# The last two units of an attention-and-FFN kernel: which thirds of x are turned by DMA, where one eviction stands, and when row sums are made

## The chip, the cores and the metric

The kernel runs on one core of one Trainium2 chip. A core has five engines that run side by side and meet through semaphores: TensorE (PE in the profile; its weight loads are shown apart as PEld), VectorE (DVE), ScalarE (ACT), GpSimd (POOL) and SyncE (SP, which here only issues DMAs). The metric is the device time of one execution in microseconds; less is better. A run is told by the median of its executions, and one execution is profiled. The profile's span is the time from the first to the last instruction of the program.

## The reference

Two blocks, one behind the other. First an attention with a hash mask: a query may see a key only if the signs of six projections agree. Then a gated FFN with RMS norm on the result, 3072 rows of 512.

```python
# B, H, S, D = 4, 8, 768, 64
mask = q_bucket[:, :, :, None] == k_bucket[:, :, None, :]      # sign bits of q @ proj, k @ proj
scores = np.where(mask, scale * np.matmul(q, k.transpose(0, 1, 3, 2)), -1000000000.0)
attn = softmax(scores)                                          # + 1e-09 in the denominator
x = np.matmul(attn, v).transpose(0, 2, 1, 3).reshape(B * S, H * D)

rms = np.sqrt(np.mean(x * x, axis=-1, keepdims=True) + 1e-06)
xn = x / rms * rms_g
g = xn @ w_gate
silu = g * (1.0 / (1.0 + np.exp(-g)))
out = (silu * (xn @ w_val)) @ w_out
```

## The kernel before

**Units and slots.** The work is cut into 8 units of 384 rows: unit `u` is half of batch element `u // 2`, and its 384 rows are three thirds `c` of 128. A unit's attention is 8 heads of 3 chunks, so 24 slots (`NS`). In a slot PE makes the scores of the next chunk (`scores`, L345, tile `s_ps`, two buffers) and ACT the exponentials of this one (`probs`, L357, tile `psb`). Everything else is filled into the slots by a plan: `plan[t]` is a list of steps, run in its order behind the scores and exponentials of slot `t`. All engines take their instructions in the order in which the plan emits them.

**What a unit goes through.** `av` (L370) multiplies the exponentials with v into `o_ps`, two heads (a pair) in one tile, of which there is one buffer. `attn_out` (called by `o_step`) empties it: DVE adds a constant and writes `otmp` (L384), takes reciprocals `rcp` (L389), and POOL multiplies into `x` (L391) and squares into `sq` (L397). `sumsq` (called by `s_step`, L413) sums the rows of `sq` on DVE. Behind the last pair, `norm` makes the row scale (`ss` on DVE, `rstd` on POOL) and scales x to `xn` in fp16.

Then `xn` must be turned, so that features lie on partitions (`xnT`), third by third, in one of two ways. `turn_dma` (L427) issues a DMA transpose on SP's queue; for such a third `norm` multiplies the RMS weights in along the row (`grow`, L448). `turn_x` makes four TensorE transposes into a PSUM bank (L463, tile `x_ps`), and the eviction multiplies the RMS weights in (`gcol`): one instruction on DVE (L469) or, with `act=True`, four on ACT (L467); for such a third `norm` multiplies by the row scale alone (`norm_third`, L456). The table `ONDMA` says how many thirds of a unit go by DMA.

The FFN has 12 tiles `ft` of 128 hidden features. `gate` (L480, `g_ps`) and `value` (L480, `v_ps`) are four matmuls each over `xnT`, in two parts; all four read all three thirds of `xnT`. ACT makes a tanh `t` of the gate (L488), DVE makes `a` from `t` and `g_ps` (L497) and `ht` from `a` and `v_ps` (L498). `project` (L509, `y_ps`) multiplies `ht` with the output weights, 12 matmuls for a third, and `store` copies on ACT (L521) and stores on SP (L522). `g_ps`, `v_ps`, `y_ps` and `x_ps` share three PSUM banks.

**Where a unit's steps run.** In unit `u + 1`'s 24 slots run, for units below 7, `norm(u)`, the turning of its x, `project` of unit `u - 1`, and the gates and values of unit `u`. `spread` places the projections, turns and gates over the slots by weights (`SCORES`, `AV`, `PROJ`, `FEED`, `TURN`): a slot takes pieces until its share of the total weight is used. `o_step` comes one slot behind the second `av` of a pair begins, `s_step` some slots later. Where such a step falls outside the first two units, and not into slot 2 or 4 of a unit, it goes to the list `late`, which is appended to the plan behind everything that `spread` placed: it then stands behind the gates of its slot.

**The tail.** After the last slot come the last rest of the plan (the last `av` steps and the `o_step` of unit 7's last pair, on DVE) and then, written out by hand: the projections of unit 6, in between them `norm(7)` and the turning of unit 7's x by `turn_x`, then unit 7's gates and values, its projections and stores.

In the run before, unit 6's attention lies from about 222 to 257 us of the span, unit 7's from about 257 to 292 us, and the tail behind it.

Of the kernel before, what the change touches and what calls it, by code (L numbers as in the profile page):

```python
# [21 lines left out]
NF = DFF // 128  # L22
# [11 lines left out]
def kernel(  # L34
# [12 lines left out]
    nc = tc.nc  # L47
# [36 lines left out]
    def bank(name, shape=None, dt=FP32):  # L84
        return gps.tile(shape or [128, 512], dt, name=name, tag="g")
# [326 lines left out]
    def sumsq(u, hp, sq):  # L412
        nc.vector.tensor_reduce(  # L413
            out=ssp[u % 2][:, hp, :], in_=sq, op=ALU.add, axis=AX.X
        )
# [3 lines left out]

    rstds = {}  # L420

    ONDMA = {2: 2, 3: 2, 4: 2, 5: 2, 6: 3}

    def turn_dma(u, c):
        if c == 0:
            xnT[u] = npool.tile([128, 4, HALF], FP16, name="xnT", bufs=2)
        nc.sync.dma_start_transpose(  # L427
            out=xnT[u][:, :, c * 128 : (c + 1) * 128], in_=xn[u][:, c, :]
        )


    def norm_scale(u):

        ss = spool.tile([128, 3], FP32, name="ss")
        nc.vector.tensor_reduce(
            out=ss, in_=ssp[u % 2].rearrange("p h c -> p c h"), op=ALU.add, axis=AX.X
        )
        rstd = spool.tile([128, 3], FP32, name="rstd")
        nc.gpsimd.tensor_tensor(out=rstd, in0=ss, in1=mhalf, op=ALU.pow)
        rstds[u] = rstd  # L440

    def norm(u):
        if u not in rstds:
            norm_scale(u)
        xn[u] = npool.tile([128, 3, DMODEL], FP16, name="xn")
        for c in range(3 if u else 2):
            if c < ONDMA.get(u, 0):
                nc.vector.scalar_tensor_tensor(  # L448
                    out=xn[u][:, c, :], in0=x[u][:, c, :], scalar=rstds[u][:, c : c + 1],
                    in1=grow, op0=ALU.mult, op1=ALU.mult,  # L450
                )
            else:
                norm_third(u, c, nc.vector.tensor_scalar_mul)

    def norm_third(u, c, mul):
        mul(xn[u][:, c, :], x[u][:, c, :], rstds[u][:, c : c + 1])  # L456

    def turn_x(u, c, act=False):
        if c == 0:
            xnT[u] = npool.tile([128, 4, HALF], FP16, name="xnT", bufs=2)  # L460
        ps = bank("x_ps", [128, 4, 128], FP16)
        for kt in range(4):
            nc.tensor.transpose(ps[:, kt, :], xn[u][:, c, kt * 128 : (kt + 1) * 128], ident16)  # L463
        dst = xnT[u][:, :, c * 128 : (c + 1) * 128]
        if act:
            for kt in range(4):
                nc.scalar.mul(dst[:, kt], ps[:, kt], gcol[:, kt : kt + 1])  # L467
        else:
            nc.vector.tensor_mul(dst, ps, gcol.unsqueeze(2).to_broadcast([128, 4, 128]))  # L469
# [34 lines left out]
    def project(u, c, f0, f1):  # L504
        if f0 == 0:
            obank[u, c] = bank("y_ps")
        y = obank[u, c]
        for ft in range(f0, f1):
            nc.tensor.matmul(  # L509
                y, ht[u][:, ft, c * 128 : (c + 1) * 128], wo[:, ft, :],  # L510
                start=(ft == 0), stop=(ft == NF - 1),
            )

    def rows_of(u, c):
        b, half = divmod(u, 2)
        rows = out[b * S : (b + 1) * S, :].rearrange("(p c) n -> p c n", c=6)
        return rows[:, 2 * c + half if b in PARITY else 3 * half + c, :]

    def store(u, c):
        ysb = spool.tile([128, DMODEL], FP32, name="ysb", bufs=3)  # L520
        nc.scalar.copy(ysb, obank.pop((u, c)))  # L521
        nc.sync.dma_start(out=rows_of(u, c), in_=ysb)  # L522
# [65 lines left out]
    NS = 24  # L588
# [5 lines left out]
    def at(w, s, f, *a):  # L594
        plan[NS * w + s].append(lambda: f(*a))
# [125 lines left out]
    def s_step(u, hp):  # L721
# [3 lines left out]
        else:  # L725
            sumsq(u, hp, sq)

    late = []
    for n, (u, h) in enumerate(order):
        t = 3 * n + 4 - ((u, h) == (0, H - 1))  # L730
        for part in range(2):
            at(0, t + part, av, u, h, part)
        if h % 2:
            if (u, h) == (0, H - 1):

                at(0, t + 1, o_step, u, h // 2, nc.vector)
                at(0, t + 1, norm_scale, u)
                at(0, t + 1, nc.vector.tensor_scalar_mul, gcol, gcol, float(DMODEL) ** 0.5)
                at(0, t + 2, hash_only, 1, 1)
                at(0, t + 2, hash_signs, 1, 1)  # L740
                at(0, t + 2, norm, u)
                at(0, TX-1, norm_third, u, 2, nc.scalar.mul)
                at(0, TX + 1, send_pair, 1, 1)
                for c in range(3):
                    at(0, TX, turn_x, u, c, c == 2)
                continue
            if (u, h) == order[-1]:
                at(0, t + 1, o_step, u, h // 2, nc.vector)
                continue

            steps = [(t + 1, o_step), (t + (6 if h < 7 else 3), s_step)]
            for s, step in steps:
                if s < 2 * NS or s % NS in (2, 4):
                    at(0, s, step, u, h // 2)
                else:
                    late.append((s, step, u, h // 2))
# [58 lines left out]
    for u in range(7):  # L815
        gates = [
            (FEED, f is gate and part == 0, [(0, f, u, ft, part)])
            for ft in range(NF) for f in (gate, value) for part in range(2)
        ]
        if u == 0:  # L820
            t0 = TX + 1
            spread(t0, 2 * NS - t0, gates)
            continue
        t0 = NS * (u + 1)
        at(0, t0 + 4, norm, u)
        for c in range(ONDMA.get(u, 0)):
            at(0, t0 + 5, turn_dma, u, c)
        pieces = []
        for i in range(9):
            c, n = divmod(i, 3)  # L830
            steps = [(0, project, u - 1, c, 4 * n, 4 * n + 4)]
            if n == 2:
                steps.append((1, store, u - 1, c))
            pieces.append((4 * PROJ, True, steps))
            if i in (6, 7):
                thirds = ((0,), (1, 2))[i - 6]
                for c in thirds:
                    if c >= ONDMA.get(u, 0):
                        pieces.append((TURN, False, [(0, turn_x, u, c)]))
                    elif u < 6:  # L840
                        pieces.append((TURN, False, []))
        lag, after = LAGS[u - 1 : u + 1]
        spread(t0 + lag, NS + after - lag, pieces + gates)
# [6 lines left out]
    def behind_norm(t):  # L850

        return t - t % NS + 9 if 1 <= t % NS < 9 else t

    for (b, hp), (load, kturns, qturns, _) in spots.items():
# [3 lines left out]
        for w, turns in (("k", kturns), ("q", qturns)):  # L858
            for i, t in enumerate(turns):
                at(0, t, turn_dve, b, hp, w, i, len(turns))  # L860
            t = turns[-1] + 1
            at(0, t if (b, hp) == (1, 2) else behind_norm(t), cast_pool, b, hp, w)
        t = 54 if (b, hp) == (1, 2) else behind_norm(qturns[-1] + 2)
# [16 lines left out]
    for t in range(LAST, LAST + 6):  # L880
        for f in plan[t]:
            f()
    for c in range(2):
        project(6, c, 0, NF)
        store(6, c)
    norm(7)
    project(6, 2, 0, 4)
    for c, f0, f1 in ((0, 4, 6), (1, 6, 8), (2, 8, NF)):
        turn_x(7, c, c == 1)
        project(6, 2, f0, f1)  # L890
    store(6, 2)
    for ft in range(NF):
# [37 lines left out]
```

## Time and profile before

| | us |
|---|---|
| median of 3 runs | 328.9 (328.4 to 329.17) |
| the profiled execution | 328.83 |
| its span | 326.7 |
| PE busy in the span | 321.3 (98%) |
| ACT, DVE, POOL busy | 228.3, 231.2, 157.6 |

PE's mean granted clock is 1.000. Rows of the timeline show start, length, engine, line, operation, what it writes and reads, and how many instructions were merged; in brackets stands the idle time of the engine before it and what ended it, if that was more than a little. A matmul's length covers its run through the array, so that one can start while the one before is still shown: the distance of starts is what a matmul costs in a stream. SPq are DMA issues on SP's queue. The page's table by engine and 40 slices is read like this: each digit is the busy share in tenths.

```profile
PE   8999999999999999999999999999999999999996
...
DVE  5887876859888559874888568885766536675870
ACT  6999887667688667776777677787777767744322
POOL 3999759955974363731873521752682220221000
```

### The profile page before, as it was taken

To read this page: it belongs to the slowest core of one execution; us is meant where nothing else is said; L and a number is where in the kernel's file an instruction comes from. 1 tells how busy PE (TensorE), PEld (TensorE's weight loads), DVE (VectorE), ACT (ScalarE), POOL (GpSimd) and SP (SyncE) were. 2 spreads that over 40 slices of the span, in tenths; PEclk is the share of its full clock that TensorE was granted. 3 is DMA by queue.
4 is the path that set the end of the run, shared out by engine and by line. 5 is a ranking of instruction groups with operands and counts; after the bars stand their busy time and mean duration, and the time that the engine had idled before them with its cause. 6 is when DMAs were issued, how large, how long until landed. Compare 5 with 4: busy or idle time off the path is not lost.

```text
span 326.7 us, 7791 instructions
## 1 busy us (share of the span) xinstructions
PE 321.3 (98%) x2955; PEld 194.1 (59%) x2955; DVE 231.2 (71%) x515; ACT 228.3 (70%) x332; POOL 157.6 (48%) x204
## 2 busy tenths in 40 slices
PE   8999999999999999999999999999999999999996
PEld 3576666656565565655566565655666556665554
DVE  5887876859888559874888568885766536675870
ACT  6999887667688667776777677787777767744322
POOL 3999759955974363731873521752682220221000
PEclk9999999999999999999999999999999999999999
DMA  7952999989328828343547047002100040002002
GB/s 216 353 163 69 230 216 200 181 138 182 102 39 155 152 79 154 54 98 99 91 102 141 9 138 135 7 1 69 68 5 3 7 127 14 2 2 90 8 2 96
DMA packets 85741, 32.63 MB, mean 100 GB/s; under 512 B 70908, under 2 KB 82632, under 8 KB 85704
## 3 DMA queue, kind: packets, MB, share of 16 engines
q1 hardware_dynamic: 81800, 27.35, 36.1%
q0 software_dynamic: 3680, 4.72, 8.6%
q8 instruction: 23, 0.38, 0.5%
q14 instruction: 14, 0.11, 0.1%
q10 hardware_dynamic: 224, 0.07, 0.1%
HBM read 28.58 MB, written 6.29 MB: 107 GB/s over the span
## 4 chain that ended last, share of the span: by engine, by line
PE 95%; DMA 2%; ACT 1%; SPq 1%; issue 0%
PE s_ps L345 20%; PE g_ps L480 19%; PE v_ps L480 19%; PE y_ps L509 17%; PE o_ps L370 11%; PE d_ps L216 2%; PE t_ps L156 2%; PE d_ps L236 2%; DMA qn<-in_q_dram 1%; PE x_ps L463 1%; ACT psb L357 1%; PE y_ps L528 1%; DMA xnT<-xn 1%; PE m_ps L329 1%; PE z_ps L576 1%; SPq L427 0%
## 5 line engine op out<-in xcount | busy, mean ns | idle before, releaser
L357 ACT ACTIVATE psb<-s_ps,ebias 128x768 f16<-128x768 f32 x192 | 168.1, 901 | 21.2 <-PE s_ps L345 20.4
L345 PE MATMUL s_ps<-QK 128*128 128x384 f16 (+1 forms) x384 | 93.5, 326 | 1.3 <-ACT psb L357 1.1
L488 ACT ACTIVATE t<-g_ps 128x384 f32<-128x384 f32 x96 | 47.3, 492 | 51.9 <-PE g_ps L480 50.2
L480 PE MATMUL g_ps<-xnT,wg 128*128 128x384 f16 x384 | 82.5, 326 | 0.2 <-DMA xnT<-xn 0.2
L480 PE MATMUL v_ps<-xnT,wv 128*128 128x384 f16 x384 | 81.8, 326 | 0.0
L497 DVE SCALAR_TENSOR_TENSOR a<-t,g_ps 128x384 f32<-128x384 f32 x96 | 53.0, 552 | 28.8 <-ACT t L488 27.3
L391 POOL TENSOR_TENSOR x<-otmp,rcp 128x384 f32<-128x384 f32 x30 | 25.1, 837 | 97.8 <-DVE rcp L389 97.6
L509 PE MATMUL y_ps<-wo,ht 128*128 128x512 f16 x276 | 67.9, 379 | 0.0
L498 DVE SCALAR_TENSOR_TENSOR ht<-a,v_ps 128x384 f16<-128x384 f32 x96 | 53.2, 554 | 12.1 <-PE v_ps L480 4.1
L370 PEld LDWEIGHTS <-psb 128*128 128x128 f16 x1152 | 51.8, 97 | 16.1 <-issue 1.2
L370 PE MATMUL o_ps<-vl,psb 128*128 128x65 f16 x1152 | 55.8, 193 | 0.1
L345 PEld LDWEIGHTS <-QK 128*128 128x128 f16 (+1 forms) x384 | 34.8, 98 | 34.9 <-issue 9.3
L480 PEld LDWEIGHTS <-wg 128*128 128x128 f16 x384 | 35.1, 97 | 21.8 <-issue 0.6
L480 PEld LDWEIGHTS <-wv 128*128 128x128 f16 x384 | 35.1, 97 | 20.7 <-issue 0.2
L509 PEld LDWEIGHTS <-ht 128*128 128x128 f16 x276 | 24.8, 98 | 22.8
L521 ACT COPY ysb<-y_ps 128x512 f32<-128x512 f32 x23 | 13.5, 587 | 17.5 <-PE y_ps L509 17.5
L384 DVE TENSOR_TENSOR otmp<-o_ps,cvb 128x390 f32<-128x390 f32 x32 | 17.9, 558 | 9.8 <-PE o_ps L370 9.8
L208 POOL CAST QK<-qT 64x768 f16<-64x768 f32 x20 | 16.5, 823 | 10.4 <-DVE qT L195 9.5
L397 POOL TENSOR_TENSOR sq<-x 128x384 f32<-128x384 f32 x24 | 19.9, 827 | 1.9
L208 POOL CAST QK<-kT 64x768 f16<-64x768 f32 x20 | 16.4, 822 | 4.6 <-DVE kT L195 2.5
L195 DVE STREAM_TRANSPOSE kT<-kL 128x192 f32<-128x192 f32 x32 | 16.5, 521 | 0.0
L195 DVE STREAM_TRANSPOSE qT<-qL 128x192 f32<-128x192 f32 x32 | 16.3, 526 | 0.0
(85 smaller groups left out, 267.5 us busy)
## 6 DMA issues: line engine op xcount, KB each, us to landing
vn<-in_v_dram SPq DMA_DIRECT2D x16, 384.0 KB
out_dram<-ysb SPq DMA_DIRECT2D x23, 256.0 KB
qL<-in_q_dram SPq DMA_DIRECT2D x40, 96.0 KB
kL<-in_k_dram SPq DMA_DIRECT2D x40, 96.0 KB
kn<-in_k_dram SPq DMA_DIRECT2D x5, 384.0 KB
qn<-in_q_dram SPq DMA_DIRECT2D x5, 384.0 KB
wg<-in_moe_w_gate_dram POOLq DMA_DIRECT2D x2, 768.0 KB, 9.5
wv<-in_moe_w_val_dram POOLq DMA_DIRECT2D x2, 768.0 KB, 11.9
```

Of the source, the lines that this page charges most:

```text
L195: nc.vector.transpose(dst.rearrange("p (c t r) -> p r c t", c=6, r=4)[:, r], src.rearrange("p (r c) d -> p r c d", r=4)[:, r],)
L208: nc.gpsimd.tensor_copy(QK[b, 2 * hp + hh, "h"][0:64, o : o + S], src[64 * hh : 64 * hh + 64, :])
L345: nc.tensor.matmul(ps[:, j, 0:HALF], QK[b, h, "h"][rows, S + jt * 128 : S + (jt + 1) * 128], QK[b, h, "h"][rows, half * HALF : (half + 1) ...
L357: nc.scalar.activation(psb[u, h][:, 2 * ch : 2 * ch + 2, :], sps.pop((u, i))[:, :, 0:HALF], AF.Exp, bias=ebias, scale=ESCALE,)
L370: nc.tensor.matmul(o[:, c, hh, 0:65], psb[u, h][:, jt, c * 128 : (c + 1) * 128], vls[b % 2][:, h, 2 * (jt % 3) + jt // 3 if b in PARITY el ...
L391: eng.tensor_mul(xd.rearrange("p c (h d) -> p c h d", h=2), tmp[:, :, :, 0:64], r.to_broadcast([128, 3, 2, 64]),)
L397: eng.tensor_mul(sq, xd, xd)
L480: nc.tensor.matmul(ps, w[:, kt, fs], xnT[u][:, kt, :], start=(kt == 0), stop=(kt == 3))
L488: nc.scalar.activation(t, fbank[u, ft, "g_ps"], AF.Tanh, scale=0.5)
L497: nc.vector.scalar_tensor_tensor(out=a, in0=t, scalar=1.0, in1=g, op0=ALU.add, op1=ALU.mult)
L498: nc.vector.scalar_tensor_tensor(out=ht[u][:, ft, :], in0=a, scalar=0.5, in1=vv, op0=ALU.mult, op1=ALU.mult)
L509: nc.tensor.matmul(y, ht[u][:, ft, c * 128 : (c + 1) * 128], wo[:, ft, :], start=(ft == 0), stop=(ft == NF - 1),)
```

## The change

Four things are done in one edit.

1. `ONDMA`: of unit 6, two thirds are turned by DMA instead of three; the last is turned by `turn_x` with the eviction on DVE, as a piece of weight `TURN` in unit 7's slots. Of unit 7, the first third is turned by DMA instead of by TensorE. Through the same table `norm` scales these thirds in the way that goes with each.
2. The tail: `norm(7)` stands behind unit 6's first projection instead of its second; it scales only two thirds, and the last is scaled on ACT. The DMA transpose is issued there. Of the two thirds that remain for `turn_x`, the second is evicted on DVE and the last on ACT, with four projection matmuls between them.
3. `AHEAD`: `o_step` of unit 6's second pair (heads 2 and 3) is put into its slot's list at once and so stands ahead of that slot's gates, instead of behind them through `late`.
4. `s_step` of unit 7's first three pairs comes 4 slots instead of 6 behind the begin of the pair's last `av`; for the third pair that is still inside the unit's slots instead of in the tail.

```diff
-    ONDMA = {2: 2, 3: 2, 4: 2, 5: 2, 6: 3}
+    ONDMA = {2: 2, 3: 2, 4: 2, 5: 2, 6: 2, 7: 1}
...
-        for c in range(3 if u else 2):
+        for c in range(3 if 0 < u < 7 else 2):
...
+    AHEAD = {(6, 1)}
...
-            steps = [(t + 1, o_step), (t + (6 if h < 7 else 3), s_step)]
+            steps = [(t + 1, o_step), (t + (3 if h == 7 else 4 if u == 7 else 6), s_step)]
             for s, step in steps:
-                if s < 2 * NS or s % NS in (2, 4):
+                if s < 2 * NS or s % NS in (2, 4) or (step is o_step and (u, h // 2) in AHEAD):
                     at(0, s, step, u, h // 2)
...
-    for c in range(2):
-        project(6, c, 0, NF)
-        store(6, c)
+    project(6, 0, 0, NF)
+    store(6, 0)
     norm(7)
+    norm_third(7, 2, nc.scalar.mul)
+    turn_dma(7, 0)
+    project(6, 1, 0, NF)
+    store(6, 1)
     project(6, 2, 0, 4)
-    for c, f0, f1 in ((0, 4, 6), (1, 6, 8), (2, 8, NF)):
-        turn_x(7, c, c == 1)
+    for c, f0, f1 in ((1, 4, 8), (2, 8, NF)):
+        turn_x(7, c, c == 2)
         project(6, 2, f0, f1)
     store(6, 2)
```

## The prediction

> **What bounds the kernel now.** I read first the page's busy times and the chain that ended last, then the timeline at the three places that the change touches, then the chain in order of time there, and last the order of instructions in the two built programs, engine by engine.
>
> The page:
>
> ```profile
> span 326.7 us, 7791 instructions
> ...
> PE 321.3 (98%) x2955; PEld 194.1 (59%) x2955; DVE 231.2 (71%) x515; ACT 228.3 (70%) x332; POOL 157.6 (48%) x204
> ...
> PE 95%; DMA 2%; ACT 1%; SPq 1%; issue 0%
> ```
>
> TensorE (PE) is the path. No other engine is near full, so a change is worth what it takes out of PE's own work or out of its few pauses. A pause is found by pitch. In the chain in order of time two 128x384 matmuls (s_ps, or half a gate) take 0.33 us until the next group starts, four take 0.65, four 128x512 (y_ps) 0.86, nine o_ps 0.27, four transposes (x_ps) 0.22. Where the next group starts later than that, PE stood still.
>
> First place, in unit 6's attention: the timeline of VectorE (DVE) and of PE (start, length, engine, line, what; in brackets the idle time before and what ended it):
>
> ```profile
> 239.84 0.56 DVE L497 SCALAR_TENSOR_TENSOR a<-t,g_ps 128x384 f32<-128x384 f32 x1 [1.24 <-ACT t L488]
> 240.50 0.56 DVE L498 SCALAR_TENSOR_TENSOR ht<-a,v_ps 128x384 f16<-128x384 f32 x1
> 240.97 0.56 DVE L384 TENSOR_TENSOR otmp<-o_ps,cvb 128x390 f32<-128x390 f32 x1
> ```
>
> ```profile
> 241.07 0.49 PE L345 MATMUL s_ps<-QK 128*128 128x384 f16 x2
> 241.68 0.43 PE L370 MATMUL o_ps<-vl,psb 128*128 128x65 f16 x9
> ```
>
> The o_ps at 241.68 is due behind the scores at 241.07 + 0.33 = 241.40. It writes the one o_ps bank, which otmp empties only at 241.53. Pause: 0.28.
>
> Second place, where unit 6's gates begin: PE, ScalarE (ACT), and a row of the chain in order of time, the last DMA transpose from issue to landing:
>
> ```profile
> 267.46 0.49 PE L345 MATMUL s_ps<-QK 128*128 128x384 f16 x2
> 268.16 0.81 PE L480 MATMUL g_ps<-xnT,wg 128*128 128x384 f16 x4 [0.22 <-DMA xnT<-xn]
> ...
> 271.31 0.81 PE L480 MATMUL v_ps<-xnT,wv 128*128 128x384 f16 x4
> 272.25 0.48 PE L345 MATMUL s_ps<-QK 128*128 128x384 f16 x2
> ```
>
> ```profile
> 270.91 0.49 ACT L488 ACTIVATE t<-g_ps 128x384 f32<-128x384 f32 x1 [0.61 <-PE g_ps L480]
> 271.30 1.69 ACT L357 ACTIVATE psb<-s_ps,ebias 128x768 f16<-128x768 f32 x2
> ```
>
> ```profile
> 265.58 2.45 DMA xnT<-xn
> ```
>
> The gate is due at 267.46 + 0.33 = 267.79 and starts at 268.16: 0.37 lost to the third DMA transpose. The scores at 272.25 are due at 271.96: 0.29 lost, since their bank is freed by a psb (from 271.30, 0.90 long) that stood on ACT behind the t at 270.91, and that t behind its gate.
>
> Third place, the tail, where unit 7's x is turned: PE, then the evictions on ACT and DVE:
>
> ```profile
> 297.60 0.39 PE L463 MATMUL x_ps<-ident,xn 128*128 128x128 f16 x4
> ...
> 299.13 1.03 PE L509 MATMUL y_ps<-wo,ht 128*128 128x512 f16 x4
> 300.08 0.82 PE L480 MATMUL g_ps<-xnT,wg 128*128 128x384 f16 x4
> ```
>
> ```profile
> 298.68 1.15 ACT L467 ACTIVATE xnT<-x_ps,gcol 128x128 f16<-128x128 f16 x4 [1.16 <-PE x_ps L463]
> ```
>
> ```profile
> 299.33 0.69 DVE L469 TENSOR_TENSOR xnT<-x_ps,gcol 128x512 f16<-128x512 f16 x1 [0.62 <-PE x_ps L463]
> ```
>
> Three groups of transposes stand there, 0.22 each, and the gate, due at 299.13 + 0.86 = 299.99, waits 0.09 for the last eviction.
>
> **The change, part by part.** All times are on the clock of the kernel before; each part shifts what follows as a whole.
>
> *One otmp ahead.* In the built order otmp and rcp of unit 6's second pair now stand before the a at 239.84. Their o_ps ends at 238.52 + 0.44 = 238.96, so they run from 238.99 to about 239.8, inside DVE's idle 1.24 us, and a still starts when t is there. Gain 0.28, cost 0. GpSimd's multiply that reads otmp keeps its place behind that engine's casts, at 242.29. If a were pushed back, the v matmuls that need its bank at 240.74 have 0.34 to spare (a ends at 240.40). Behind this place everything up to unit 7 hangs on PE: the QK rows sent by DMA from 238.16 on land by 244.5, the scores that read them start at 247.8. So the 0.28 should last. Bounds: 0 to 0.28; I take 0.28, since I find no wait that would swallow it.
>
> *Unit 6: two thirds by DMA, the last on PE.* Removed: one DMA issue on SyncE (SP), 1.22 us, and with it the wait of 0.37, since the second transpose landed at 266.72 by its semaphore, 2.45 after an issue at 264.27. SP's two stores behind it go out 1.3 us sooner; nobody waits for them. Added on PE: four transposes, 0.22, behind the o_ps at 266.32, so from 266.60 (0.39 to their end). Their eviction on DVE runs 267.02 to 267.71; the gate is now due at 267.79 + 0.22 = 268.01, so 0.3 is to spare. Unit 5 is turned in just this way in the kernel before (x_ps at 229.55, eviction at 229.97, gate at 230.96 with no idle time named). The otmp that stood at 266.80 falls behind the eviction, to 267.71 to 268.27; the o_ps that needs its bank comes at about 269.3. The scaling of that third is a plain scalar multiply of 0.48 in place of 0.75, off the path. Sum: +0.22 - 0.37.
>
> *The new order in unit 7's slots.* The extra piece of weight 220 moves the gates between slots. In the built order the second gate is cut in two halves around a pair of scores, and on ACT the psb of the scores before stands ahead of that gate's t. So: first gate 268.01 to 268.82, its t at 268.85, psb 0.39 later from 269.24 to 270.14, next psb from 270.03 to 270.93. The scores that need the first psb are due at 270.23, those that need the second at 271.81. The wait of 0.29 is gone, with a margin of only 0.09 at the first. Bounds: 0 to 0.29 gained; I take 0.29.
>
> *Tail.* One group of transposes less: -0.22 on PE. Now y, four of them, lie between the two groups: first x_ps at 297.60, second at 298.68, gate due at 299.77. The second group is evicted by ACT: from 299.11, four pieces, the first done after 0.38 and the others 0.26 apart (1.15 in all): 299.49, 299.75, 300.01, 300.26. In the built order each of the gate's four matmuls waits for its own piece; they are due at 299.77, 299.93, 300.10, 300.26, so only the last waits, about 0.04. The old wait of 0.09 is gone. ACT comes to the first t at about 300.67 instead of 300.94, which matters, because the tail's v matmuls are paced by t and a (v at 302.07 starts as a of 301.46 + 0.56 ends). Sum: -0.22 - 0.09 + 0.04 = -0.27.
>
> The scaling that moved to ACT (0.73, as the one such row) fits between the copies at 294.34 and 296.93. The new DMA transpose is behind one store on SP. The first third is scaled from 295.98 before; the row sums of unit 7's third pair (all three pairs move; 0.55 at 292.21, in front of otmp at 292.67) now stand ahead of the last gate's a, so everything is 0.46 sooner: scaling from 295.52, done after 0.75 at 296.27, issued at 296.34. By their semaphores the first transposes of units 2 to 5 landed 2.47 to 2.61 us after the issue, unit 6's 3.17 (its issue took 2.01, the others' 1.2 to 1.3). So it lands between 298.8 and 299.5, before 299.77. The row sums are thus worth nothing on the path; without them the slow landing would cost 0.2. Unit 6's second store, behind the transpose on SP, is ready at 297.52 and goes out at most 0.9 later; only the last stores, 20 us on, would matter. Bounds of the tail: -0.31 to +0.3 (the slow landing with as much again on top, 3.17 + 0.7, is 0.54 past 299.67).
>
> [...]
>
> Sum: -0.28 + 0.22 - 0.37 - 0.29 - 0.27 = -0.99. The profiled execution took 328.83 for its span of 326.7; what lies around the span is untouched. 328.83 - 0.99 = 327.84; the median of the runs, 328.9, stands 0.07 above that execution. I say 327.9.
>
> **Rivals.**
>
> *The waits come back elsewhere.* The margins are 0.09 at unit 7's scores and about 0.3 at the tail. If one more psb falls behind a t (-0.29 lost) and the tail gains nothing (-0.27 lost), 0.43 is left: 328.4. For it: ACT's order is fixed and this wait came from it. Against: worked through, each wait has its room.
>
> *The transpose of unit 7 is late.* The gates need it by about 299.67, 3.33 after its issue. Beyond that each us is a us; from 4.3 on the kernel is slower than before. If each of its four blocks took the 1.22 that SP now spends on a whole third, it would land 4.9 after the issue, 1.55 late: 327.84 + 1.55 = 329.4. For it: unit 6's first one, on a queue that had been quiet, was 0.6 longer than the rest, and the tail's is alike. Against: ten of eleven landed within 2.61. [...]
>
> *It does little.* PE may stand for something that the semaphores do not tell, and the shifts are used up before the end; only the tail's 0.27 stays: 328.6.
>
> **How the numbers follow.** Forecast 0.68, waits come back 0.17, little 0.07, late transpose 0.08. A measurement of this kernel tells about 0.2% from no change, 0.66 us here, so faster means under 328.2. The forecast is 0.99 with some 0.3 of spread between runs (328.4 to 329.17 before), so nearly all of it is faster; with a little of the second case: faster 0.70. The rest of the second, the third: same 0.20. Slower 0.10. Low end: the sum with the runs' spread below, 327.3. High end: the second case and the same spread, 328.8; what is left out is the late transpose and part of the third.
>
> **What would show it.** In the profile after: the o_ps after unit 6's second pair directly behind its scores; no gate of unit 6 released by a DMA and four x_ps more in front of it; no scores that wait for psb in unit 7's slots; in the tail two groups of x_ps, and a gate 2.2 us and not 2.5 behind the first. Wrong would be: a gate in the tail released by the DMA xnT, scores released by psb, or x_ps in unit 7 that wait for a bank.

## The result

| | before | after |
|---|---|---|
| median, side by side (5 runs each) | 328.4 us (327.74 to 329.17) | 327.47 us (327.12 to 327.66) |
| ratio | | 0.9961 [0.995, 0.9972] |
| the profiled execution | 328.83 | 327.66 |
| its span | 326.7 | 325.9 |
| time less span, that execution | 2.13 | 1.76 |

The change makes the kernel 0.39% faster, 1.28 us by the ratio. The ratio on record is not the quotient of the two medians: these differ by 0.93 us (0.28%), which is the edge of its interval. In the experiments below the kernel before was run 31 to 33 times beside each group and stood at 328.74 to 328.94, so the five runs of the table, with 328.4, were on its low side.

The page of the changed kernel (span, busy times, and the shares of the chain that ended last):

```profile
span 325.9 us, 7789 instructions
...
PE 321.1 (99%) x2954; PEld 194.6 (60%) x2955; DVE 231.0 (71%) x514; ACT 228.6 (70%) x333; POOL 157.6 (48%) x204
...
PE 98%; ACT 1%; issue 0%
```

PE's busy time fell by 0.2 only, and it is busy 99% of the span where it was 98%. The 2% of DMA and 1% of SPq, which the chain of the kernel before had, are gone. Only a part of that is the change's: of the DMA rows 2.45 us were the third transpose of unit 6, and 3.04 us a load of q at the very start (`qn<-in_q_dram`), which the edit does not touch and which stands in the chain again, with 4.76 us, in a later profile of the changed kernel with two memsets more. The three places follow, in the timeline of the changed kernel.

First place, VectorE and then PE:

```profile
239.14 0.56 DVE L384 TENSOR_TENSOR otmp<-o_ps,cvb 128x390 f32<-128x390 f32 x1 [0.40 <-PE o_ps L370]
239.74 0.19 DVE L389 RECIPROCAL rcp<-otmp 128x6 f32<-128x6 f32 x1
239.99 0.55 DVE L497 SCALAR_TENSOR_TENSOR a<-t,g_ps 128x384 f32<-128x384 f32 x1
```

```profile
241.22 0.49 PE L345 MATMUL s_ps<-QK 128*128 128x384 f16 x2
241.54 0.44 PE L370 MATMUL o_ps<-vl,psb 128*128 128x65 f16 x9
```

The otmp and rcp lie in what was DVE's idle time, a follows with no named wait, and the o_ps starts 0.32 behind the scores where it was 0.61.

Second place, PE and then ACT:

```profile
266.47 0.39 PE L463 MATMUL x_ps<-ident,xn 128*128 128x128 f16 x4
266.69 1.03 PE L509 MATMUL y_ps<-wo,ht 128*128 128x512 f16 x4
267.56 0.49 PE L345 MATMUL s_ps<-QK 128*128 128x384 f16 x2
267.88 0.81 PE L480 MATMUL g_ps<-xnT,wg 128*128 128x384 f16 x4
...
271.03 0.81 PE L480 MATMUL v_ps<-xnT,wv 128*128 128x384 f16 x4
271.68 0.49 PE L345 MATMUL s_ps<-QK 128*128 128x384 f16 x2
```

```profile
268.73 0.49 ACT L488 ACTIVATE t<-g_ps 128x384 f32<-128x384 f32 x1 [0.39 <-PE g_ps L480]
269.12 1.69 ACT L357 ACTIVATE psb<-s_ps,ebias 128x768 f16<-128x768 f32 x2
```

The four transposes cost 0.22 (266.47 to 266.69). The gate stands 0.32 behind its scores, the scores at 271.68 stand 0.65 behind the v_ps: both pauses are gone, and ACT runs the two psb in a row behind one t.

Third place, the tail: PE, ACT, and the DMA issues on SP's queue:

```profile
297.03 0.39 PE L463 MATMUL x_ps<-ident,xn 128*128 128x128 f16 x4
297.26 1.03 PE L509 MATMUL y_ps<-wo,ht 128*128 128x512 f16 x4
298.12 0.39 PE L463 MATMUL x_ps<-ident,xn 128*128 128x128 f16 x4
298.34 1.03 PE L509 MATMUL y_ps<-wo,ht 128*128 128x512 f16 x4
299.21 0.85 PE L480 MATMUL g_ps<-xnT,wg 128*128 128x384 f16 x4
299.90 0.81 PE L480 MATMUL v_ps<-xnT,wv 128*128 128x384 f16 x4
```

```profile
298.54 1.14 ACT L467 ACTIVATE xnT<-x_ps,gcol 128x128 f16<-128x128 f16 x4 [1.59 <-PE x_ps L463]
```

```profile
296.13 1.26 SPq L427 DMA_TRANSPOSE xnT<-xn  x1
```

Two groups of x_ps and no wait before the gate. The gate takes 0.69 instead of 0.65 until the value starts, the 0.04 for the last of ACT's four pieces. The transpose landed, by its semaphores, at 298.63, 0.58 before the gate.

The starts of the same matmuls in the two traces tell what each place gave: the o_ps moved by -0.29 against what went ahead of it, the x_ps put +0.23 in, the gate gave -0.38, the scores -0.29, the tail -0.24. That is -0.97. Another 0.16 was lost in the first 83 us, in slots that the change does not touch, so the span is only 0.8 shorter. Most of it, 0.14, lies at one place: the scores at 82.96 start that much late, and in three other of the fourteen profiles the same scores are late by 0.32, 0.45 and 1.41, in the other ten by nothing. The rest of the 1.17 between the two executions, 0.37, lies outside the span.

### The profile page after: what moved, and what is told of

It reads as the page before. It is cut to its first block, busy times and chain, and to the rows that moved or that the text cites. A ratio compares the mean times of both kernels' runs of the same rounds, so it can differ in the third digit from the quotient of the medians.

```text
span 325.9 us, 7789 instructions
## 1 busy us (share of the span) xinstructions
PE 321.1 (99%) x2954; PEld 194.6 (60%) x2955; DVE 231.0 (71%) x514; ACT 228.6 (70%) x333; POOL 157.6 (48%) x204
## 4 chain that ended last, share of the span: by engine, by line
PE 98%; ACT 1%; issue 0%
PE s_ps L345 20%; PE g_ps L480 19%; PE v_ps L480 19%; PE y_ps L509 18%; PE o_ps L370 11%; PE d_ps L216 2%; PE t_ps L156 2%; PE d_ps L236 2%; PE z_ps L576 1%; PE x_ps L463 1%; PE y_ps L528 1%; PE m_ps L329 1%; ACT psb L357 1%; PE s_ps L156 0%; ACT ypart L533 0%
## 5 line engine op out<-in xcount | busy, mean ns | idle before, releaser
L469 DVE TENSOR_TENSOR xnT<-x_ps,gcol 128x512 f16<-128x512 f16 x11 | 7.4, 688 | 15.0 <-PE x_ps L463 14.9
```

## The experiments

In the one trace the span's part had come as forecast. The first eight kernels ask whether each pause is worth on the clock what it shows in a trace, and whether its cause is the one named; the last four ask about what lies outside the span, a question that the 0.37 above raised and the results of the eight sharpened. The kernels were timed in three groups, each beside the kernel before. Where a ratio stands below, it is to the kernel before of the same group, and kernels of two groups are compared by their ratios.

### The kernel before, and each part alone

**The kernel before once more** (no edit):

> The kernel before, unchanged, beside itself. The profiled executions went from 328.83 to 327.66, 1.17 less, of which 0.8 is span; time less span was 2.13 before and 1.76 after. Theory sample: the 328.83 and the median 328.9 of three were a high sample; here the median comes out at 328.4 +/- 0.4, ratio 1.000 +/- 0.0015, and time less span lies near 1.8 in most executions. Rival surround: the change took 0.4 outside the span; then time less span is 2.1 in every execution of this kernel and 1.76 in those of kernels with the new tail.

Measured: 328.83 (328.39 to 329.54, 11 runs) against 328.74 (33 runs), ratio 1.0004 [0.9995, 1.0013]. The first theory, a high sample, put the median at 328.4 +/- 0.4 and time less span near 1.8. It failed: the median is 328.83 and that of time less span 2.04, near the rival's 2.1. A ratio of eleven runs holds about 0.1%, 0.3 us, which is the size of one part of this change. The part kernels are therefore read in their traces first.

**The otmp ahead alone:**

```diff
+    AHEAD = {(6, 1)}
...
-                if s < 2 * NS or s % NS in (2, 4):
+                if s < 2 * NS or s % NS in (2, 4) or (step is o_step and (u, h // 2) in AHEAD):
```

> Only the otmp of unit 6's second pair ahead of its gates. Theory pauses: the o_ps due at 241.40 starts there, the pause of 0.28 is gone and nothing takes it up later: span 0.28 less, ratio 0.9991. All other pauses stay: 0.37 at unit 6's first gate (DMA xnT), 0.29 at the scores that wait for psb, 0.09 at the tail's gate. Rival swallowed: the 0.28 comes back at a later wait before unit 7 or grows the 0.37 to 0.65, ratio 1.000.

Measured: 328.46, ratio 0.9988 [0.998, 0.9997], -0.39 with an interval of -0.66 to -0.10. In the trace the pause of 0.28 is gone and the other three stand, the one at unit 6's first gate with 0.15 instead of 0.37 (why is told below). The gain holds alone and lasts to the end.

**Unit 6 alone:**

```diff
-    ONDMA = {2: 2, 3: 2, 4: 2, 5: 2, 6: 3}
+    ONDMA = {2: 2, 3: 2, 4: 2, 5: 2, 6: 2}
```

> Only ONDMA of unit 6 from 3 to 2. Theory pauses: +0.22 for four transposes, -0.37 for the wait on the DMA, -0.29 for the scores that waited for psb: -0.44, ratio 0.9987. The pause at 241.68 (0.28) and the tail's 0.09 stay. Rival waits come back: scores wait for psb in the new order, or the gate waits for the eviction on DVE: -0.15 at most, ratio 0.9995.

Measured: 328.72, ratio 0.9996 [0.9987, 1.0005], -0.13 with an interval of -0.43 to +0.16. The trace shows both pauses gone, the pauses at unit 6's second pair and in the tail untouched, and the last matmuls 0.46 sooner than in the profile of before. So the trace gives the forecast in full and the clock hardly a third of it. Two things explain that without a new stall. The pause at the gate is not 0.37 in most executions (below), and the span ends 2.87 instead of 2.79 behind the last matmul, for a reason that the tail shows more strongly. With these, +0.22 - 0.26 - 0.29 + 0.08 = -0.25, which the interval holds.

**The tail alone**, with the row sums as in the change:

```diff
-    ONDMA = {2: 2, 3: 2, 4: 2, 5: 2, 6: 3}
+    ONDMA = {2: 2, 3: 2, 4: 2, 5: 2, 6: 3, 7: 1}
...
-            steps = [(t + 1, o_step), (t + (6 if h < 7 else 3), s_step)]
+            steps = [(t + 1, o_step), (t + (3 if h == 7 else 4 if u == 7 else 6), s_step)]
...
-    for c in range(2):
-        project(6, c, 0, NF)
-        store(6, c)
+    project(6, 0, 0, NF)
+    store(6, 0)
     norm(7)
+    norm_third(7, 2, nc.scalar.mul)
+    turn_dma(7, 0)
+    project(6, 1, 0, NF)
...
```

> Only the tail: unit 7's first third by DMA, the new order of projections and turns, row sums of unit 7 two slots sooner; unit 6 still three thirds by DMA. Theory pauses: -0.22 for four transposes less, -0.09 for the old wait, +0.04 for the last piece of ACT's eviction: -0.27, ratio 0.9992, the DMA landing before the gate is due. Rival late transpose: the gate in the tail is released by the DMA xnT, ratio 1.000 or above. Rival surround: time less span falls by 0.3 to 0.4 beside the kernel before, so that the ratio is 0.998.

Measured: 328.56, ratio 0.9999 [0.9988, 1.0009]. PE's gain of the tail is there: no wait before the gate, the transpose landed 2.43 after its issue. But the span's end comes 3.26 behind the last matmul and not 2.79. What SP's queue waited for from 320 us on, in the changed kernel and then in this one (in all, times, longest):

```profile
SPq L930 <- DMA out_dram<-ypart: 1.4, 3, 0.6
```

```profile
SPq L928 <- DMA out_dram<-ypart: 1.9, 1, 1.9
```

L930 and L928 are the kernel's last line, where SP waits for the semaphores of its DMAs one after the other. In the changed kernel, as in the one before, these waits meet the stores in the order in which they land, and the last one ends the row. In this kernel the first wait is for the store that lands last, and seven more semaphore instructions, 0.065 apart, come behind it: 0.46. It has one DMA more than either, twelve transposes and not eleven. Unit 6 alone has one DMA less, ten transposes: there one such instruction comes behind the last store's wait, which is its 0.08. The tail alone thus comes to nothing on the clock, by a sum of -0.24 on PE, +0.47 at the span's end and -0.22 outside the span, where its median is 1.81 against 2.03 (below). The rival's fall of time less span came, but not its ratio of 0.998.

### The scores' wait for psb and the order on ACT

Two kernels test whether the wait of the scores for psb comes from the order that the piece's weight makes, as the forecast said, or from anything else in unit 6's transposes. In the first, unit 6 keeps three thirds on DMA, and only an empty piece of the same weight is added to the kernel before; in the second, the changed kernel keeps its x_ps but the piece weighs nothing.

```diff
-                    elif u < 6:
+                    elif u < 6 or c == 2:
                         pieces.append((TURN, False, []))
```

> The kernel before with one empty piece of weight 220 where the changed kernel has the turn of unit 6's last third; all three thirds still by DMA. Theory order: the wait of 0.29 at unit 7's scores hangs on where the gates fall between the slots, so it goes without any TensorE transpose, while the gate still waits 0.37 for the DMA: -0.29. Rival start: the wait went because the first gate starts sooner and not in the DMA's shadow; then it stays here, 0.00.

```diff
-                        pieces.append((TURN, False, [(0, turn_x, u, c)]))
+                        pieces.append((TURN if u < 6 else 0, False, [(0, turn_x, u, c)]))
```

> The changed kernel, but the turn of unit 6's last third has weight 0 in the plan, so that the gates fall into the slots as before. Theory order: the second gate is whole again, its t stands on ACT ahead of the psb of the scores before, and scores due at about 271.8 (the clock of the kernel before) wait 0.28 for that psb: 0.28 above the changed kernel. Rival start: no such wait, 0.00 against the changed kernel.

Measured: 328.68, ratio 0.9997 [0.9986, 1.0008], for the first; 328.13, ratio 0.998 [0.9964, 0.9996], for the second. PE in the first, and in the second PE and then ACT:

```profile
267.94 0.49 PE L345 MATMUL s_ps<-QK 128*128 128x384 f16 x2
268.77 0.81 PE L480 MATMUL g_ps<-xnT,wg 128*128 128x384 f16 x4 [0.35 <-DMA xnT<-xn]
...
271.92 0.81 PE L480 MATMUL v_ps<-xnT,wv 128*128 128x384 f16 x4
272.57 0.49 PE L345 MATMUL s_ps<-QK 128*128 128x384 f16 x2
```

```profile
270.54 0.81 PE L480 MATMUL v_ps<-xnT,wv 128*128 128x384 f16 x4
271.48 0.48 PE L345 MATMUL s_ps<-QK 128*128 128x384 f16 x2
```

```profile
270.14 0.49 ACT L488 ACTIVATE t<-g_ps 128x384 f32<-128x384 f32 x1 [0.61 <-PE g_ps L480]
270.53 1.69 ACT L357 ACTIVATE psb<-s_ps,ebias 128x768 f16<-128x768 f32 x2
```

The weight alone takes the wait away (0.65 from v_ps to the scores in the first), and without the weight it is back (0.94 in the second, 0.29 lost), with t again ahead of the psb. In the first the wait is gone although its gate starts later than in the kernel before, so a sooner start is not what removes it: the order is the cause. This stands on the traces. On the clock the first has -0.10 with an interval of -0.46 to +0.26, which holds -0.29 and nothing as well; the second is 0.43 slower than the changed kernel by the later of its two ratios (0.9980 against 0.9967), with intervals that overlap.

The first also shows a gate that waits 0.50 for the third transpose. That wait can be read in every kernel that still turns three thirds of unit 6 by DMA: SP's three issues in a row, and the gate's start less the scores' start less 0.33.

| kernel | SP's three issues, us | gate late by, us |
|---|---|---|
| tail alone | 4.22 | 0.00 |
| otmp ahead alone | 4.42 | 0.15 |
| before, again | 4.50 | 0.24 |
| two memsets off VectorE (below) | 4.53 | 0.27 |
| before | 4.63 | 0.37 |
| empty piece | 4.77 | 0.50 |

The two ends of it, on SP's queue:

```profile
262.37 4.22 SPq L427 DMA_TRANSPOSE xnT<-xn  x3
```

```profile
262.64 4.77 SPq L427 DMA_TRANSPOSE xnT<-xn  x3
```

The second and third issue take 1.21 to 1.22 in all six; what varies is the first, from 1.61 to 2.15, and from 4.42 on the gate follows it one for one. So the wait belongs to an execution, not to the kernel: 0.26 in the mean of six, where the prediction took one profile's 0.37.

### The transpose in the tail

The first of two kernels undoes the fourth edit alone (row sums as before, everything else as changed). The second issues the transpose behind unit 6's second projection and store.

```diff
-            steps = [(t + 1, o_step), (t + (3 if h == 7 else 4 if u == 7 else 6), s_step)]
+            steps = [(t + 1, o_step), (t + (6 if h < 7 else 3), s_step)]
```

> The changed kernel with unit 7's row sums 6 slots behind as before. Forecast: everything in norm(7) is 0.46 later, the DMA transpose lands about 299.1 instead of 298.6 on the changed kernel's clock, its gate is due at 299.2 and the weight load about 0.1 before: 0.00 to 0.1 against the changed kernel, and 0.2 to 0.3 only if the landing is the slow one (2.8 to 3.2). Rival: the row sums are what makes the tail work, and the gate now waits 0.3 or more for DMA xnT in any case.

```diff
-    turn_dma(7, 0)
     project(6, 1, 0, NF)
     store(6, 1)
+    turn_dma(7, 0)
```

> The changed kernel with the DMA transpose of unit 7's first third issued behind the store of unit 6's second third, so behind a copy that ends about 297.0 on the changed kernel's clock, and a store's issue of about 0.4 to 0.5. Theory: it is issued at about 297.5 instead of 296.1, lands 2.5 later at 300.0, the gate due at 299.2 starts at 300.1: +0.9 against the changed kernel, one for one. Rival: other work or the tail's slack takes part of it up, +0.5 or less.

Measured: 327.62, ratio 0.9969 [0.9954, 0.9984], for the late row sums; 328.42, ratio 0.9995 [0.9982, 1.0009], for the late transpose. PE in the one and in the other, and the issue in the other:

```profile
299.48 1.03 PE L509 MATMUL y_ps<-wo,ht 128*128 128x512 f16 x4
300.48 0.81 PE L480 MATMUL g_ps<-xnT,wg 128*128 128x384 f16 x4
```

```profile
298.32 1.03 PE L509 MATMUL y_ps<-wo,ht 128*128 128x512 f16 x4
299.98 0.81 PE L480 MATMUL g_ps<-xnT,wg 128*128 128x384 f16 x4 [0.63 <-DMA xnT<-xn]
```

```profile
297.41 1.25 SPq L427 DMA_TRANSPOSE xnT<-xn  x1
```

With the row sums late, the transpose is issued at 297.70 of that execution, landed at 300.35, and the gate is 0.14 behind its due time: a little, and not to be told apart on the clock. That profile ran 328.89, the slowest of its ten runs, for another reason: scores that the edit does not touch, due at 82.00 + 0.65 = 82.65, waited 1.41 for a transfer.

```profile
82.00 0.81 PE L480 MATMUL v_ps<-xnT,wv 128*128 128x384 f16 x4
84.06 0.48 PE L345 MATMUL s_ps<-QK 128*128 128x384 f16 x2 [1.25 <-DMA QK<-bits]
```

With the transpose itself 1.28 later the gate waits 0.80. On the clock the late transpose is 0.80 slower than the late row sums of the same group, and 0.9 to 1.1 slower than the changed kernel by the ratios (0.9995 against 0.9967 and 0.9961). So the cover in the tail is what the trace shows, about 0.5, and beyond it the trace loses us for us; the clock agrees within its spread.

### Outside the span

The kernels fell into two groups by their time less their span (medians over the runs): 2.02 to 2.06 for the kernel before, the otmp ahead, unit 6 alone and the empty piece; 1.76 to 1.81 for the changed kernel, the tail alone and the three that vary the changed kernel. Single executions overlap a little: with the runs below, ten of 150 of the first group read 1.74 to 1.86, and the second group reaches 1.86. The one trace of each kernel does not tell what those ten had. In the traces of the first group a DMA packet of the kind instruction, called the fetch below, follows 1.8 us behind the span's end; the second group has none. DMA from 326.6 to 333 us in the kernel before (its span ends at 326.7), and from 327 to 335 in the changed one:

```profile
DMA packets 1, 0.01 MB, mean 1 GB/s; under 512 B 0, under 2 KB 0, under 8 KB 0
...
q14 instruction: 1, 0.01, 0.6%
```

```profile
DMA packets 0, 0.00 MB, mean 0 GB/s; under 512 B 0, under 2 KB 0, under 8 KB 0
```

What separates the groups in all ten traces is the number of VectorE's instructions with its semaphore instructions: 699 in the first, 697 in the second. No other engine's number does so: ScalarE has 479 to 481 and SP 359 to 363 without relation, GpSimd 263 in all. The change takes two away, a scaling that moved to ScalarE and one wait for a semaphore. So the idea was that these two instructions decide whether the fetch comes behind the program's end. Four kernels were run together for that and for the order of the last waits.

> The changed kernel once more, unaltered, beside the three that follow. The theory now stands at -1.15 us in sum: -0.28 (otmp ahead), +0.22 (x_ps in unit 6), -0.26 (mean of the wait for the third transpose over five executions), -0.29 (psb), -0.26 (tail), and -0.28 outside the span (time less span was 2.05 in before and about 1.77 after). So a ratio of 0.9965 +- 0.001, span 325.5 to 326.0, time less span 1.7 to 1.9. If the 0.9961 of the first measurement was partly chance and nothing happens outside the span, the ratio would be 0.9974 or more and time less span 2.0.

```diff
-    mhalf = const.tile([128, 3], FP32, name="mhalf")
+    mhalf = const.tile([128, 3], FP32, name="mhalf"); idle1 = const.tile([128, 1], FP32, name="idle1")
...
-    project_part(7, 2, 0, 256, nc.scalar.copy, nc.sync)
+    nc.vector.memset(idle1, 0.0); nc.vector.memset(idle1, 1.0); project_part(7, 2, 0, 256, nc.scalar.copy, nc.sync)
```

> The changed kernel with two small memsets more on VectorE, placed where VectorE has been idle for 6 us in front of its last copy, so that nothing in the span can wait for them. Theory: the 0.28 outside the span hangs on the length of VectorE's instruction stream (699 rows in the trace where an 8 KB instruction fetch starts 1.8 us behind the span's end, 697 where none does). Then the fetch is back behind the end, time less span is about 2.05, and the time is 0.28 above c0_after_again (ratio to before about 0.997 to 0.9975) at the same span. Rival: the fetch comes from something else that the tail's edit changes (the number of DMAs or of ScalarE's instructions); then nothing changes against c0_after_again (within 0.1 us).

```diff
-    nc.vector.memset(ebias, EBIAS)
-    nc.vector.memset(mhalf, -0.5)
+    nc.gpsimd.memset(ebias, EBIAS)
+    nc.gpsimd.memset(mhalf, -0.5)
```

> The kernel before with two memsets of small constants at the start given to GpSimd instead of VectorE: two instructions less on VectorE (697 rows), nothing else moved. Theory of the instruction stream's length: no fetch behind the span's end, time less span about 1.77, time 0.28 below before (ratio 0.9991) at an unchanged span of about 326.7 to 327.5. Rival: ratio 1.000, fetch and 2.05 stay.

```diff
-    store(6, 2)
+    ysb = spool.tile([128, DMODEL], FP32, name="ysb", bufs=3)
+    nc.scalar.copy(ysb, obank.pop((6, 2)))
+    rows = rows_of(6, 2)
+    nc.sync.dma_start(out=rows[:64], in_=ysb[:64])
+    nc.sync.dma_start(out=rows[64:], in_=ysb[64:])
```

> The changed kernel with the store of unit 6's last third cut into two halves of 64 rows, one DMA more in all, far from the end (it lands some 18 us before). Theory from a3_tail_only, which had one DMA transpose more and a span's end 3.26 instead of 2.79 us behind the last matmul: SyncE's last waits go through the DMA semaphores in a fixed order, and one DMA more turns the order so that the semaphore landing last is waited for first and seven more waits of 0.065 us follow. Then the span's end comes 3.2 to 3.3 us behind the last matmul and the time is about 0.47 above c0_after_again. Rival: the 3.26 had another cause, and this kernel ends 2.8 behind its last matmul, at the time of c0_after_again (within 0.15 us).

Measured, beside 31 runs of the kernel before at 328.94:

| kernel | median | ratio | time less span | fetch behind the end |
|---|---|---|---|---|
| before | 328.94 | | 2.06 | yes |
| changed, again | 327.74 | 0.9967 [0.9952, 0.9981] | 1.78 | no |
| changed, two memsets more | 327.66 | 0.9963 [0.9949, 0.9976] | 2.00 | yes |
| before, two memsets less | 328.41 | 0.9987 [0.9978, 0.9995] | 1.79 | no |
| changed, a store cut in two | 328.19 | 0.9979 [0.9969, 0.9989] | 1.79 | no |

DMA from 326.6 to 333 us in the changed kernel with two memsets more, then in the kernel before with two less:

```profile
DMA packets 1, 0.01 MB, mean 1 GB/s; under 512 B 0, under 2 KB 0, under 8 KB 0
...
q14 instruction: 1, 0.01, 0.4%
```

```profile
DMA packets 0, 0.00 MB, mean 0 GB/s; under 512 B 0, under 2 KB 0, under 8 KB 0
```

Both go as the theory of the instruction stream's length says: two instructions more on VectorE bring the fetch back and put 0.22 on what lies outside the span; two fewer in the kernel before take it away, and 0.27 with it. The store cut in two has one DMA more and no fetch, so the number of DMAs is not what brings it. The 14 packets on this queue inside the span of the kernel before (0.11 MB) are of 8 KB, as the one behind it is. Why two instructions decide over one packet more was not shown. One expectation failed: the time of the changed kernel with two memsets more was to be 0.28 above its twin, the changed kernel run again, and it is 0.08 below. Its span stands at 325.60 in the median of 12 runs, the twin's at 325.95 of 8, and both are 326.0 in the profile; spans of one kernel spread over 1 us, so the total cannot show 0.22 here, while time less span, which spreads far less, can. For the same reason the 0.43 by which the kernel with two less beats the kernel before (ratio 0.9987, interval 0.16 to 0.72 us) is not all the fetch's: 0.27 lie outside the span, the rest inside it, where nothing was forecast.

The store cut in two is 0.45 slower than its twin, and its span ends 3.24 behind the last matmul instead of 2.79: 0.45 again, as expected of one DMA more.

## Why the prediction was right and wrong

The forecast was 327.9, 0.99 less than before; measured were 327.47 and, by the ratio, 1.28 less.

**Right: the four places and their mechanisms.** Forecast against the trace after: otmp ahead -0.28 against -0.29; four x_ps +0.22 against +0.23; scores and psb -0.29 against -0.29; the tail -0.27 against -0.24, with the 0.04 at the last of ACT's pieces where it was forecast (the forecast's own times put that piece and its matmul both at 300.26, so the size of that wait did not follow from them). The two kernels with and without the weight show that it is the order on ACT that frees the scores. The row sums were put at nothing on the path, and undoing them costs 0.14 in the trace at most.

**Wrong: "what lies around the span is untouched".** This is the step that failed. The sum was made inside the span and carried over to the time as if the 2.13 outside it in the profiled execution stayed. That part fell too, by 0.25 in the medians (2.03 to 1.78), because the edit leaves VectorE two instructions shorter (697 and not 699), and with them the fetch behind the program's end goes away (one packet before, none after). Nothing in the list of costs would have found it: no engine's busy time and no wait in the span shows it. The packet itself stands in the trace of before, 1.8 us behind the span's end, but nothing there says that it hangs on two instructions.

**Mis-sized: the wait for the third transpose.** The mechanism was right, the 0.37 is the value of one execution. Six executions of kernels with that wait show 0.00 to 0.50 with a mean of 0.26, since SP's first issue there takes 1.61 to 2.15. The trace after shows -0.38 only because it was compared with that same execution.

With both, the sum is -0.28 + 0.22 - 0.26 - 0.29 - 0.27 - 0.25 = -1.13. The two measurements of the change give -1.28 (0.9961) and -1.09 (0.9967), so it fits both; -0.99 is inside their intervals too, but made of a term 0.11 too large and one 0.25 too small, and that these work against each other is luck.

**The rivals.** The waits did not come back: the margin of 0.09 at unit 7's scores held in the trace. The late transpose did not happen, and its price was real: moved by 1.28, it took 0.80 in the trace and with that most of the gain. The 4.9 us from issue to landing that this rival reckoned with appeared nowhere: unit 7's third landed 2.41 to 2.65 after its issue in the eight traces that have it, 2.50 in that of the changed kernel. That the change does little was excluded by the ratio, but its idea of gains used up before the end had a core of truth in the parts alone: the tail alone loses its 0.24, and what it saves outside the span, to the order of SP's last waits, and the whole change does not, since a third less by DMA in unit 6 and one more in unit 7 leave the number of DMAs as it was. The prediction did not price that, and that it was right at zero for the whole change is the luck of this balance.

## What to carry to other kernels

When gains are a few tenths of a us, count the ends of the program as part of the path: here one DMA more or less changed at which of SP's last semaphore waits the last store landed (0.45 us for one more, 0.08 for one less), and two instructions on VectorE added or removed a fetch behind the end (0.22 to 0.28 us). Take the size of a pause from several executions before it goes into a sum, since one on a transfer's issue moved between 0 and 0.5 us, and one on a transfer far from the edit between 0 and 1.41. And give a part of a change its worth only together with the parts that it shares a counter with: the tail's edit alone was worth nothing.

## What the runs showed of the hardware

- A DMA packet of 8 KB of the kind instruction, 1.8 us behind the span's end, comes and goes with two VectorE instructions, and the time outside the span with it (2.00 to 2.06 with, 1.76 to 1.81 without). That the packet itself is what costs the 0.25, and not something that goes with it, was not tested apart.
- In the kernel before and in the changed one SP's waits on the last line meet the stores in the order in which they land, and the span ends 2.79 us behind the last matmul. In the two kernels with one DMA more the first of these waits, 1.9 us long, is for the store that lands last, and the span ends 3.26 (the tail alone) and 3.24 us (the store cut in two) behind the last matmul; in the tail alone seven more semaphore instructions, 0.065 us apart, stand behind that wait. In the kernel with one DMA less (unit 6 alone) one such instruction stands behind it, and the span ends 2.87 us behind the last matmul.
- The first DMA transpose of unit 6 takes SP 1.61 to 2.15 us to issue in the six profiles of the table above and 1.69 in that of the changed kernel, where the other transposes of the kernel before take 1.20 to 1.33 and unit 7's 1.25 to 1.37. Why that one varies stays open.
